# State products of a decayed delta rule: 40 stationary columns over cleared rows, and another order of the steps

## The chip, the cores and the metric

The kernel runs on one core of one Trainium2 chip. The metric is device microseconds (us) of the whole program. A core has TensorE (PE in the profile; its loads of the stationary operand are a row of their own, PEld), VectorE (DVE), ScalarE (ACT), GpSimd (POOL) and SyncE (SP), which issues nearly all DMAs. TensorE reads both operands from SBUF and writes to PSUM.

## What is computed

For each of 4 x 8 heads a 40 x 40 state is carried over 768 tokens; the outputs then pass a small gated network.

```python
for t in range(S):
    y[:, :, t] = einsum('bhd,bhde->bhe', rt, state)
    Sa = einsum('bhde,bhe->bhd', state, at)
    state = state * wt[:, :, None, :] - einsum('bhd,bhe->bhde', Sa, bt) \
            + einsum('bhd,bhe->bhde', vt, kt)
# x: (4, 768, 320), all heads' y side by side
h = maximum(x @ w_in, 0)                 # 320 -> 1024
conv_out = 3-tap convolution of h along the tokens, a weight per channel
out = (h * sigmoid(conv_out)) @ w_out    # 1024 -> 320
```

All arrays are f32, and so are nearly all products.

## The kernel before, in words

The 768 tokens are cut into 24 steps of 32 tokens; two steps make a pair (12 pairs, `pds`) and also a window of the network (12 windows, `wds`). Each unit of work is a Python generator that issues some instructions and then yields: `load_wakb`, `decays`, `decayed`, `scores`, `solve_in`, `solve` per pair or step (they prepare the triangular systems of a step), `chain` (the recurrence), `hats`, `vturn`, `rturn`, `sturn`, `pairs`, `from_state`, `outputs`, `finish` (the attention output), `moe_pack`, `moe_in`, `moe_out` (the network) and the 23 pieces that decode the weights from 64-bit floats on DVE, seven instructions a piece (`wi..`, `wo..`, `wp..`, `cv` in tile names).

`ORDER` is a written list of 1990 tokens, such as `ch5*2`: "advance unit chain 5 by two yields". The order of tokens is the order of instructions on every engine and queue; nothing else schedules them. An engine takes its instructions in that order, so an instruction that waits holds all that stand behind it on its engine.

The recurrence of step n is `chain(st, nxt)`: products `pp` of the old state with `a64` (line 592) and of `vu` with `at` (line 603); a copy to `psb`; products `pu` with `tt`, the solved system (line 618); copies of `pu` into `vu` on ACT (line 631) and DVE (line 629); then the **state product** `pn` (line 644); the DVE addition to the old state (line 655, line 653 in step 0); and the POOL multiplication by the decay (line 660), on which the next step's line 592 waits. There are 23 state products: the last step has none.

The state lies in rows 0 to 39 (even heads) and rows 64 to 103 (odd heads) of `states`; line 655 works on all of rows 0 to 103. Each state product has, per head, two batches `y` and two row halves `z` (partitions 0 to 63 and 64 to 127 of `kb` and `vu`), 32 products of 40 moving columns, each of which appears as two instructions in the profile. For even heads the stationary operand has 64 columns (`m = D if x else 64`, D being 40): the 24 further ones belong to the next head and fill rows 40 to 63 of `pn` with finite numbers that nobody uses, so that line 655 reads nothing that was never written. For odd heads it has 40.

`solve` is 62 instructions that depend on one another, on DVE for the pairs whose letter in `SOLVER` is v and on POOL for the others. Its input goes through DRAM (`bd`, then `bb`), and so does its output (`xd`, then `tt`).

Of the kernel before, what the change touches and what calls it, by code (L numbers as in the profile page):

```python
# [39 lines left out]
st1 we9 st1 we5 so1 dd2 pa0 si1 we9 ld2 we10 vt0 ch1*2 so1 vt1 dd2 pa0 vt1 ou0 rt0 we9 so1 we10 ld2  # L40
we10*2 dd2 so1*2 dd2*2 ch1 lr1 dd2 ou0*2 ld2 we11 we12 lv2 we6 ch1 sc4*2 ha2 we10 sc4 sc5 ld3 st1
pa0 ha2 fs1 we11*2 sc5 de2 we12 de2 fs1 de2 fi0 pa1 so1 vt1 we13 ha2 ha3 fi0 ch1*2 ha3 de3*2 ld3
we9 pa1 ou1 rt1 we12 fi0 ha3 fi0 dd2 fi0 we13 si2 ou1 ch2 fi1 ou1 we12 rt1 fi1 st2 pa1 we14 ch2 de3
st2 de3 so1 fi1 so1 so2 we11 ch2 ha4 fi1 so2 we15 ch2 we14 ch2 fs2 ha4 de3 we15 ch2*2 vt2 we16
ro0*2 pk0 mi0.0 so2 st2 rt1 fs2 lv3 ch2 vt2 so2 we16 mi0.0 dd3 ch2 mi0.1 ha4 we17 ch3 dd3 so2 we17
mi0.0 ch3*2 mi0.1*2 ld3 st3 mi0.0*2 we18 st3 lv2 ch3 de3 ch3 pa2 dd3 vt2 ld3 ha5 we19 ld3 vt3 pa2
vt3 ld4 fi1 ou2 vt3 we18 ch3 we19 st3 ou2 lr2 ha5 ch3 so2 mi0.1 pa2 mi0.1 lv4 mi0.1 mi0.2 dd3 mi0.1
ou2 fs3*2 pa3 ha5 dd3*2 so2 we20 we21 pa3 lv5 mi0.3 fi2 ou3 fi2 dd3 sc5 so2 fi2 mi0.1 lv1 ou3 mi0.0
ch3 sc6 mi0.3*2 ch3 st4 mi0.0 sc6 so2 we20 si2 fi2 st4 ch4*2 sc6 ch4 mi0.3 fi2 mi0.0 fi3 rt2 mi0.0
fi3*2 mi0.3 rt2 we21 dd3 mi0.2*2 sc7 ch4 sc7 we22 de4 lr0 ch4*2 lr1 mi0.2 we2 mi0.3 ch4 mi0.2*2  # L50
we22 mi0.2 mi0.3*2 mi0.2 mo0.1 we20 mi0.1 fi3 pk1 mo0.1 de4 vt4 mi1.0 mi1.1*3 si3 lv3 mi0.3 ou3
mi1.0 ch4 ld4 lv5 ld4 so2 de4 mo0.0 mi1.0 so3*2 mi1.1*2 so3 ch4 fi3 sc7 we14 ld4 pa3 lv6 st4 fs4
ch5*2 vt4 mo0.1 dd4 mi1.1 mi1.0 si3 mi1.0 we16 we1 pk1 vt4 ch5 so3*3 mo0.1 mi1.1 lr3 dd4*2 mi0.2
mi1.1 fs4 ha6 pa4 ld4 mi1.3 pa4 ha6 dd4*3 ou4 mi1.3 dd4 mo0.1*2 mi1.3 st5 so3 pa4 st5 ld5 mo0.0
we18 dd4 mi1.3 sc8 mi1.0 sc8 mi1.3 sc8 mi1.0 sc9 ou4 ro0 sc9 ch5*2 st5 mi1.0 mi1.2*3 mi1.3 so3
vt5*2 mi1.2*2 si4 ou4 ch5 so3 mi1.2 ch5 mo0.0 ha6 ha7 mo0.0 ha7 ch5 fs5*2 pa5 mi1.2 sc9 mo0.0 mi1.2
ch5 de4*3 fi4 de5 mi1.3 mo0.0 pa5 so3 de5 ou5 so4 rt2 ou5 de5 fi4*2 mi1.3 fi4 mo1.1 rt3 fi4 mo1.0
fi5 rt3 vt5 fi5*3 ch6*2 ou5 pa5 mo1.1*2 de5 so4 ch6*2 de5 ch6 st6 mo1.0 st6 ch6 pk2 mi1.3 vt6 mo1.1
so4 we12 mi1.2 mi2.2*2 lv7 ch6*3 lv8 so4 vt6 ha7 ch7 fs6*2 pa6 ld5 st6 so4 mo1.0 pa6 si4 mi2.2 st7
ld5 we7 mi1.0 fi5 rt3 ch7 st7 ch7 so4 ld5 mi2.3*3 vt6 ha8 ou6 so4 ha8 so4 ou6 mo1.1 ch7*2 dd5*2 we8  # L60
ch7*2 dd5 ou6 pa6 ch7 mi2.2 mi2.3 fi6*2 mi1.1 vt7 dd5 mi2.0 mi2.2 vt7 fi6*3 we3 fs7 ch7 vt7 mi2.3
ch8 mi2.2*2 pk0 lr4 dd5 mi2.2 ha8 fs7 ch8*2 dd5 mi2.0*2 mo1.0 so4 dd5 de5 mi2.3 sc10*3 sc11 st7
mi2.0 ld5 ld6 mi2.0 st8 mi2.3 sc11 ha9 ch8 ld6 st8 we13 st8 mi2.0 ch8 mi2.3 ha9 pa7 de6 si5 pa7 ld6
lv9 de6 ch8*2 pa7 ou7*2 sc11 dd5 ch8 so4 rt4 de6 fi7 lr4 fi7*2 rt4 vt8 fi7 so5*3 mo1.1 vt8 pk3
mi2.1*4 ou7 so5 mi2.1*2 lv9 dd6 mi2.0 mi2.1*2 ld6 fs8*2 pa8 we15 lv8 ha9 mo1.0 vt8 we22 ld6 ld7 de6
mo1.0 mi2.1 de6 pa8 mi2.0 mi2.2 si5 mi3.1*3 mi3.2 ch8 ch9*2 dd6*2 de6 so5*2 ch9 mo2.1 pk2 dd6*3
mi3.2 mi3.1 we21 ou8 dd6 mi3.1 mi3.2 mi3.1 ou8 we17 dd6 lv10 st9*2 sc12*2 st9 pa8 sc12 sc13 mi2.3
fi7 ld7 sc13 ch9 mi3.1 rt4 ch9 so5 lr5 mi3.2 ou8 mi3.1 de7*3 mi3.3 fi8 mi3.3*2 vt9 mo2.1 si6 ha10
fi8 vt9 mi2.0 fs9*2 pa9 so5*2 ch9 mi3.3*2 mi3.2 fi8 so5 we19 pa9 ha10 mo2.1*2 ou9 ch9*2 vt9 ou9*2
lv6 fi8 mo2.1 fi8 mi3.2*2 ha10 rt5 mi3.0 mo2.0 so6 mi3.2 rt5 mo2.1 mi3.0 ld7 lr2 ch9 mi3.0 fi9  # L70
ch10*3 so6 mo2.0 st10 mi3.2 mi3.0*2 mo2.0 ch10 st10 ld7 ha11 fi9 mi3.3 fi9 ch10 mi3.0 ch10 ha11
ch10 mi3.1 mi3.0 so6 ha11 fi9 mi3.3 mo2.0 mi3.3 pk4 ch10 lr3 vt10 lv11 dd7 ch10 fs10 vt10 mi3.0
ch11 mi3.0 mi3.3 mi4.0*3 mo3.1*2 mi4.0 dd7 so6*2 mi4.0 ch11 vt10 mi4.0 lr6 so6 pa9 mi4.2*3 ch11
fs10 dd7 fi9 de7 ld7 mo2.0*2 de7 ch11 mi4.0 ch11 st10 ha12 st11*2 mi4.2 pa10*2 mo3.1 ha12 pa10
mi4.2 so6 dd7 ou10 mi4.2 ch11 ou10 mi4.3 mo3.1 de7 mo3.0 rt5 fi10 dd7 so6 fi10*3 ch11 fi10 we11
# [926 lines left out]
```

## Time and profile before

| | |
|---|---|
| median of 3 runs | 658.02 us (656.59 to 660.3) |
| the profiled execution | 654.06 us |
| its span, first to last instruction | 652.3 us |
| PE busy | 565.5 us, 87% of the span |
| DVE, POOL, ACT busy | 474.7, 289.7, 281.0 us |
| mean granted TensorE clock, as a share of full speed | 0.922 |

The profile is of one execution, so sums of its rows stand against 654.06 us, of which 1.8 us lie outside the span. Matmuls are pipelined: busy PE says that some product was under way, not that the engine ran at its peak. "issue" as a releaser means that the engine waited for nothing that the profile shows. A row gives the line of the program, the engine, the operation, and out<-in by the program's names.

### The profile page before, as it was taken

The numbers are of one execution on the slowest core, as the hardware profiler recorded it, in microseconds if no ns is written. First come the engines' busy times: TensorE is split into PE (matmuls) and PEld (weight loads), VectorE is DVE, ScalarE is ACT, GpSimd is POOL, SyncE is SP. The second block draws the span as 40 slices with busy tenths as digits, with TensorE's granted clock in tenths as the row PEclk, the third lists the DMA queues.
The fourth block names the chain that finished last, engine by engine and source line by source line (L and its number), as shares of the span: only waits on it lengthen the run. The fifth ranks groups of instructions, "written<-read, shape, count | busy, mean of one in ns | idle before, by whom it ended". The sixth has DMA issues, their size and how long they took to land.

```text
span 652.3 us, 31811 instructions
## 1 busy us (share of the span) xinstructions
PE 565.5 (87%) x14385; PEld 486.4 (75%) x14385; DVE 474.7 (73%) x977; ACT 281.0 (43%) x578; POOL 289.7 (44%) x530
## 2 busy tenths in 40 slices
PE   3536677888799999989998998988999998999998
PEld 2535566787688788877887887867977887788884
DVE  7899978789968987767975458966658985254552
ACT  2112223355436254545525446514535426456562
POOL 5030488884786211884012772010687125851000
PEclk9866687798989998989997999989999988999999
DMA  9592835582923566534522652552763522120011
GB/s 145 80 155 35 154 65 115 127 149 56 122 53 70 89 110 96 96 72 73 92 51 59 95 93 49 80 98 41 114 88 70 95 53 55 39 55 21 12 26 31
DMA packets 214400, 51.89 MB, mean 80 GB/s; under 512 B 203729, under 2 KB 208809, under 8 KB 214265
## 3 DMA queue, kind: packets, MB, share of 16 engines
q1 hardware_dynamic: 210104, 49.20, 44.3%
q8 instruction: 113, 1.85, 1.2%
q10 hardware_dynamic: 4160, 0.66, 0.8%
q14 instruction: 23, 0.18, 0.1%
HBM read 38.30 MB, written 10.22 MB: 74 GB/s over the span
## 4 chain that ended last, share of the span: by engine, by line
PE 40%; POOL 23%; DVE 21%; issue 9%; DMA 6%; SPq 1%; ACT 0%; POOLq 0%; DVEq 0%; ACTq 0%
POOL st L560 11%; PE po L846 10%; POOL xx L566 9%; PE ph L799 9%; DVE xx L566 4%; DVE st L560 4%; PE pm L709 2%; PE ps L498 2%; DVE cc L828 2%; PE pu L618 2%; DMA bb<-bd 2%; PE pn L644 2%; DVE k L481 2%; PE pt L694 1%; DMA bd<-at 1%
## 5 line engine op out<-in xcount | busy, mean ns | idle before, releaser
L846 PE MATMUL po<-wo,g 128*128 128x320 f32 x384 | 121.1, 452 | 0.0
L828 DVE SCALAR_TENSOR_TENSOR cc<-hb,cw,cc 128x256 f32<-128x256 f32 x192 | 93.0, 546 | 38.5 <-ACT cc L820 38.3
L560 POOL TENSOR_TENSOR st<-xx,bb 128x126 f32<-128x126 f32 (+22 forms) x217 | 100.5, 463 | 20.6 <-DMA bb<-bd 4.2
L566 POOL TENSOR_TENSOR xx<-xx,st 128x126 f32<-128x126 f32 (+22 forms) x217 | 94.7, 436 | 17.0
L846 PEld LDWEIGHTS po<-wo,g 128*128 128x128 f32 x384 | 70.3, 197 | 22.9 <-issue 2.2
L660 POOL TENSOR_TENSOR state<-state,a 104x640 f32<-104x640 f32 x23 | 36.7, 1597 | 112.4 <-DVE state L655 106.5
L776 POOL TENSOR_TENSOR xl<-xf,xh 120x384 fp32r<-120x384 f32 x24 | 28.7, 1196 | 119.3 <-ACT xf L774 119.3
L799 PE MATMUL ph<-xh,wih 120*128 120x256 f32 x288 | 74.9, 320 | 0.1
L813 ACT ACTIVATE hb<-ph 128x512 f32<-128x512 f32 x48 | 28.7, 598 | 72.8 <-PE ph L799 72.6
L799 PEld LDWEIGHTS ph<-xh,wih 120*128 120x128 f32 x288 | 50.7, 199 | 4.1 <-issue 0.5
L566 DVE TENSOR_TENSOR xx<-xx,st 128x56 f32<-128x56 f32 (+22 forms) x155 | 46.0, 297 | 5.3
L833 ACT ACTIVATE cc<-cc 128x512 f32<-128x512 f32 x48 | 29.8, 630 | 41.5 <-DVE cc L828 40.7
L560 DVE TENSOR_TENSOR st<-xx,bb 128x56 f32<-128x56 f32 (+22 forms) x155 | 42.6, 275 | 5.2
L838 DVE TENSOR_TENSOR g<-cc,hb 128x512 f32<-128x512 f32 x48 | 34.4, 722 | 13.5 <-ACT cc L833 12.9
L820 ACT ACTIVATE cc<-hb,cw 128x256 f32<-128x256 f32 x96 | 43.5, 503 | 0.0
L799 PE MATMUL ph<-xh,wil 120*128 120x256 f32 x192 | 40.5, 294 | 0.2 <-issue 0.2
L799 PE MATMUL ph<-xl,wih 120*128 120x256 f32 x192 | 40.6, 294 | 0.0
L498 PE MATMUL ps<-a,k 40*64 40x32 f32 x1536 | 30.8, 230 | 10.7 <-issue 8.1
L498 PEld LDWEIGHTS ps<-a,k 40*64 40x64 f32 x1536 | 28.4, 146 | 14.4 <-issue 11.2
L644 PE MATMUL pn<-vu,kb 64*64 64x40 f32 (+1 forms) x1472 | 30.4, 221 | 7.8 <-DVE vu L629 2.3
L644 PEld LDWEIGHTS pn<-vu,kb 64*64 64x64 f32 (+1 forms) x1472 | 26.4, 127 | 12.6 <-issue 4.3
L716 DVE TENSOR_TENSOR ms<-pm,tri 128x512 f32<-128x512 f32 x24 | 16.5, 687 | 25.8 <-PE pm L709 25.5
(286 smaller groups left out, 1186.1 us busy)
## 6 DMA issues: line engine op xcount, KB each, us to landing
bb<-bd SPq DMA_DIRECT2D x24, 256.0 KB
rin<-in_r_dram SPq DMA_DIRECT2D x48, 80.0 KB
vu<-in_v_dram SPq DMA_DIRECT2D x96, 40.0 KB
in<-in_w_dram SPq DMA_DIRECT2D x23, 160.0 KB
in<-in_a_dram SPq DMA_DIRECT2D x23, 160.0 KB
in<-in_k_dram SPq DMA_DIRECT2D x23, 160.0 KB
in<-in_b_dram SPq DMA_DIRECT2D x23, 160.0 KB
out_dram<-ob SPq DMA_DIRECT2D x44, 80.0 KB
```

The source lines that it names most:

```text
L498: nc.tensor.matmul(ps[half(z), x, (4 * y + i) * C : (4 * y + i) * C + C], pd["k64"][half(x, D), 2 * i + y, c, z], pd["a64"][half(x, D), re ...
L560: eng.tensor_tensor(t3, xx[:, 0:nj, i : i + 1].to_broadcast([128, nj, nt]), bb[:, i : i + 1, i + 1 :].to_broadcast([128, nj, nt]), ALU.mult,)
L566: eng.tensor_tensor(xx[:, 0:nj, i + 1 :], xx[:, 0:nj, i + 1 :], t3, ALU.add)
L644: nc.tensor.matmul(pn[half(x, m), z, q * D : q * D + D], kf[half(z), kp : kp + m], vu[half(z), h, y, 0:D], start=True, stop=True, skip_gro ...
L660: nc.gpsimd.tensor_tensor(new, new, al.to_broadcast([SR, 2, 8, D]), ALU.mult)
L776: nc.gpsimd.tensor_tensor(wd["xl"][:, :, :, tw], xf, xh.bitcast(F32), ALU.subtract)
L799: nc.tensor.matmul(ph[:, j], l[:, fs], x, start=(j == 0 and i == 0), stop=(i == len(passes) - 1), skip_group_check=True,)
L820: nc.scalar.activation(out=cc[:, j], in_=hb[:, j, :, 1 : W + 1], func=AF.Copy, scale=cw[:, 1, f : f + 1],)
L828: nc.vector.scalar_tensor_tensor(out=cc[:, j], in0=hb[:, j, :, x : W + x], scalar=cw[:, x, f : f + 1], in1=cc[:, j], op0=ALU.mult, op1=ALU ...
L833: nc.scalar.activation(out=cc, in_=cc, func=AF.Sigmoid)
L838: nc.vector.tensor_tensor(g, cc, hb[:, :, :, 1 : W + 1], ALU.mult)
L846: nc.tensor.matmul(po[:rows, :DM], parts(f), wo[:, f, :], start=(f == 0), stop=(f == NF - 1))
```

## The change

Every state product now has 40 stationary columns, for even heads too. As nothing fills rows 40 to 63 of `pn` any longer, two bf16 products of zeros go ahead of it, one for each row half `z`: 64 stationary columns from a new tile `zst` of zeros, and 320 moving columns of `xini`, a bf16 tile of ones and zeros that is there already. They write zeros into rows 0 to 63 of both banks; the even heads' products then overwrite rows 0 to 39.

```diff
+    zst = cp.tile([128, 64], BF16, name="zst")
+    nc.gpsimd.memset(zst, 0.0)
...
         pn = banks(f"pn{n}")
         kf = kb.rearrange("p q d -> p (q d)")
+
+        for z in range(2):
+            nc.tensor.matmul(
+                pn[half(0), z, 0:HD], zst[half(z)],
+                xini.rearrange("p s t -> p (s t)")[half(z), 0:HD],
+                start=True, stop=True, skip_group_check=True,
+            )
         for h in range(H):
             x, i = h % 2, h // 2
-            m = D if x else 64
             for y in range(2):
                 kp, q = kbp(h, y) * D, 2 * i + y
                 for z in range(2):
                     nc.tensor.matmul(
-                        pn[half(x, m), z, q * D : q * D + D],
-                        kf[half(z), kp : kp + m], vu[half(z), h, y, 0:D],
+                        pn[half(x, D), z, q * D : q * D + D],
+                        kf[half(z), kp : kp + D], vu[half(z), h, y, 0:D],
                         start=True, stop=True, skip_group_check=True,
                     )
```

The table `ORDER` is another one, with the same 1990 tokens in other places. Its first row shows the kind of difference:

```diff
-we0 ld0 we1 we0 we1 ld0 we0 ld0 de0 we2 de0 we0 de0 dd0*5 ld0 we2 dd0*2 de0 we3*2 de0 we0 sc0*3 sc1
+we0 we1 we0 ld0*3 we1 we0*2 we2 de0*3 dd0*5 we2 we3 ld0 dd0*2 de0 ld0 de0 we3 sc0*3 sc1 ld1 we2 de0
```

Lines of the changed kernel are numbered up to 7 higher. Three places show what moves.

On PE, around the state product of step 2 (`pn2`), with `py2` and `pv2` its neighbours. Before:

```order
L731 MATMUL py2_1766<-sd2_1633,r64_113 32x40 x32
L644 MATMUL pn2_1810<-vu0_117,kb2_1333 64x40 x4
L644 MATMUL pn2_1810<-vu0_117,kb2_1333 40x40 x4
L669 MATMUL pv2_1844<-ident_78,vu0_117 128x128 x8
L799 MATMUL ph00_1862<-xh0_1419,wih_127 128x256 x2
```

The two rows of `pn2` stand there four times in turn. Now:

```order
L738 MATMUL py2_1780<-sd2_1664,r64_115 32x40 x32
L641 LDWEIGHTS zst_98
L641 MATMUL pn2_1825<-xini_94,zst_98 64x320
L651 MATMUL pn2_1825<-vu0_119,kb2_754 40x40 x32
L676 MATMUL pv2_1883<-ident_78,vu0_119 128x128 x8
```

The rows of line 641 stand there twice, once for each row half. All 32 products of `kb` and `vu` have 40 columns, and the zeros are in front of them.

On PE, just ahead of the first products of step 3's chain (`pp3` from `state1`, which wait for POOL); `ph00` and `ph01` are the first products of the network. Before:

```order
L418 MATMUL pa3_1911<-ident_78,in1_107 128x128 x8
L799 MATMUL ph01_1920<-xh0_1419,wih_127 128x256 x2
L799 MATMUL ph01_1920<-xh0_1419,wil_128 128x256 x2
L799 MATMUL ph01_1920<-xl0_1420,wih_127 128x256 x2
L799 MATMUL ph01_1920<-xh0_1419,wih_127 128x256
L799 MATMUL ph01_1920<-xl0_1420,wil_128 128x256
L592 MATMUL pp3_1933<-state1_125,a641_397 32x40 x32
```

Now:

```order
L806 MATMUL ph00_1896<-xh0_1271,wih_129 128x256 x2
L806 MATMUL ph00_1896<-xh0_1271,wil_130 128x256 x2
L806 MATMUL ph00_1896<-xl0_1272,wih_129 128x256 x2
L806 MATMUL ph00_1896<-xh0_1271,wih_129 128x256
L806 MATMUL ph00_1896<-xl0_1272,wil_130 128x256
L806 MATMUL ph01_1916<-xh0_1271,wih_129 128x256 x2
L806 MATMUL ph01_1916<-xh0_1271,wil_130 128x256 x2
L806 MATMUL ph01_1916<-xl0_1272,wih_129 128x256 x2
L806 MATMUL ph01_1916<-xh0_1271,wih_129 128x256
L806 MATMUL ph01_1916<-xl0_1272,wil_130 128x256
L593 MATMUL pp3_1930<-state1_127,a641_411 32x40 x32
```

The transposes `pa3` went behind `pp3`, and the second eight products of `ph00`, which stood behind `pp3`, went ahead of it; a first group of eight stands ahead of these rows in both orders.

On DVE, at the end of pair 0's solve (`st0`, `xx0`), the second half of pair 1's scores (`at2` from `ps3`). Before:

```order
L505 TENSOR_TENSOR at2_568<-ps3_603,tris_89 128x2x2x128
L560 TENSOR_TENSOR st0_28_653<-xx0_399,bb0_361 128x45
L566 TENSOR_TENSOR xx0_399<-xx0_399,st0_28_653 128x15x3
L560 TENSOR_TENSOR st0_29_656<-xx0_399,bb0_361 128x30
L566 TENSOR_TENSOR xx0_399<-xx0_399,st0_29_656 128x15x2
L560 TENSOR_TENSOR st0_30_659<-xx0_399,bb0_361 128x16
L566 TENSOR_TENSOR xx0_399<-xx0_399,st0_30_659 128x16
L264 TENSOR_SCALAR wi21q_447<-wi21r_446 80x256
```

Now:

```order
L265 TENSOR_SCALAR wi02q_623<-wi02r_622 120x256
L269 TENSOR_SCALAR wi02q_623<-wi02r_622 120x256
L273 SCALAR_TENSOR_TENSOR wi02q_623<-wi02r_622,wi02q_623 120x256
L277 SCALAR_TENSOR_TENSOR wi02q_623<-wi02q_623 120x256
L278 TENSOR_SCALAR wi02q_623<-wi02q_623 120x256
L279 SCALAR_TENSOR_TENSOR wi02q_623<-wi02r_622,wi02q_623 120x256
L282 TENSOR_TENSOR wi02q_623<-wi02q_623 120x256
L506 TENSOR_TENSOR at2_545<-ps3_635,tris_89 128x2x2x128
L432 SCALAR_TENSOR_TENSOR suf_105<-wz_100,dp0_102 128x1056
```

`at2` from `ps3` moved from ahead of the last six instructions of the solve to behind the two weight pieces `wi21` and `wi02`.

## Rows read from the trace of the kernel before

**Rows 1.** The page: engines; PE, its clock and the DMA rate in 40 slices.

```profile
PE 565.5 (87%) x14385; PEld 486.4 (75%) x14385; DVE 474.7 (73%) x977; ACT 281.0 (43%) x578; POOL 289.7 (44%) x530
PE   3536677888799999989998998988999998999998
PEclk9866687798989998989997999989999988999999
GB/s 145 80 155 35 154 65 115 127 149 56 122 53 70 89 110 96 96 72 73 92 51 59 95 93 49 80 98 41 114 88 70 95 53 55 39 55 21 12 26 31
```

**Rows 2.** Busy time of each engine in six stretches of the span.

```profile
core 0: us, PE busy (x) PEld busy (x) DVE busy (x) ACT busy (x) POOL busy (x), PEclk, DMA share, GB/s
0.00:65.00 65.00, 31.27 (x544) 27.90 (x544) 56.58 (x139) 14.08 (x20) 16.51 (x32) 0.79 0.73 104
65.00:130.00 65.00, 49.64 (x1351) 43.56 (x1351) 53.88 (x100) 19.69 (x34) 50.00 (x99) 0.74 0.58 115
130.00:260.00 130.00, 118.47 (x3432) 103.66 (x3433) 109.55 (x220) 60.20 (x124) 66.34 (x117) 0.96 0.55 93
...
520.00:652.30 132.30, 125.60 (x2724) 103.28 (x2722) 67.35 (x141) 64.99 (x148) 39.88 (x73) 0.97 0.17 37
```

**Rows 3.** Waits of PE over the whole span: in total, times, longest, in us.

```profile
PE ps L498 <- issue: 8.1, 6, 3.0
PE pp L603 <- issue: 8.0, 3, 3.5
PE pp L592 <- POOL state L660: 7.3, 4, 4.1
PE pn L644 <- DVE vu L629: 2.3, 3, 1.9
```

**Rows 4.** Timeline of PE, single products: start, length, instructions, idle before with releaser.

```profile
592.64 1.13 PE L644 MATMUL pn<-vu,kb 64*64 64x40 f32 x64
552.96 0.79 PE L744 MATMUL py<-kb,ms 64*32 64x40 f32 x64
```

**Rows 5.** Groups by form, whole span: count, busy us, mean ns, idle before.

```profile
L644 PEld LDWEIGHTS pn<-vu,kb 64*64 64x64 f32 x736 | 26.3, 138 | 11.9 <-issue 3.6 <-DVE vu L629 3.3 <-ACT vu L631 1.5
L644 PEld LDWEIGHTS pn<-vu,kb 64*40 64x40 f32 x736 | 21.1, 117 | 0.7 <-issue 0.7
```

**Rows 6.** The chain that ended last: products of 320 and 256 moving columns.

```profile
577.20 1.08 PE po L846 x4
578.28 0.95 PE ph L799 x8
```

**Rows 7.** Timeline of PE, ACT and DVE in the first 20 us.

```profile
7.32 1.94 PE L418 MATMUL pw<-ident,in 128*128 128x128 f32 x8 [7.32 <-DMA in<-in_w_dram]
9.29 1.01 ACT L428 COPY wz<-pw 128x1024 f32<-128x1024 f32 x1 [0.43 <-PE pw L418]
12.24 2.35 DVE L431 TENSOR_TENSOR_SCAN suf<-wz,dp 128x1056 f32<-128x1056 f32 x1
```

**Rows 8.** Timeline of DVE, SP's queue and POOL, end of solve 0 to solve 1.

```profile
58.18 0.68 DVE L505 TENSOR_TENSOR at<-ps,tris 128x512 f32<-128x512 f32 x1
65.54 2.35 DVE L431 TENSOR_TENSOR_SCAN suf<-wz,dp 128x1056 f32<-128x1056 f32 x1
65.97 1.03 SPq L539 DMA_DIRECT2D bd<-at  x2
75.86 1.34 POOL L660 TENSOR_TENSOR state<-state,a 104x640 f32<-104x640 f32 x1
77.14 0.67 POOL L553 CAST xx<-xini 128x512 f32<-128x512 bf16 x1
```

**Rows 9.** Timeline of PE ahead of step 3's chain.

```profile
127.77 1.04 PE L418 MATMUL pa<-ident,in 128*128 128x128 f32 x8
131.24 0.82 PE L592 MATMUL pp<-state,a 40*32 40x40 f32 x64 [1.49 <-POOL state L660]
```

**Rows 10.** Waits of PE from 130 to 260 us.

```profile
PE pp L592 <- POOL state L660: 2.2, 2, 1.5
```

**Rows 11.** Timeline of PE at one of its longest waits on issue.

```profile
427.15 0.33 PE L731 MATMUL py<-sd,r 64*32 64x40 f32 x10 [3.30 <-issue]
428.49 3.84 PE L846 MATMUL po<-wo,g 128*128 128x320 f32 x7
```

More of the change, by code (lines that the diff above doesn't have):

```diff
@@ L40 @@
[L40 to L75, printed above, removed]
@@ new lines @@
+mi4.0 lv12 st11 dd7 mo3.0 dd7 pa10 mi4.2 we19 vt11*2 ch11 ou10 lv13*2 so6 mi4.2 pa10 mo3.1 mi4.1
+ch11*2 ou10 ha12 ch11 fi9 fi10 dd7 fi10*2 mi4.0*2 dd7 ou10 mi3.3 fs11*2 pa11 rt6*2 mi4.0 pa11 mi4.1
+mi4.2 mi4.1 ou11*2 rt6 ou11 fi10*2 sc14*2 st11 sc14 sc15*2 vt11 de7 dd7 mi4.2*3 de8*2 st12 pk3
+so6*2 st12 mi4.3*3 ha13 mi4.3 ch12*2 mo3.0 fi11 pa11 mo3.0 ch12 ha13 si6 ld8 mo3.1 fi11*2 si7*2
+mi4.1 ch12 fs12 fi11 pk5 de8 mi4.3*3 ch12 mi4.1 de8 mo3.0 de8 mi4.3*2 ch12*2 so7 ch12 st12 ld8*2
+ha13 mi5.3 so7 mi5.3*2 ch12 vt12 mi4.0 vt12 so7 mi4.1 so7 fs12 ch13 lv14 fi11 ch13*2 pa12 st13 dd8
@@ new lines @@
+mo4.0 ch14*2 mi5.1 lr8 ha16*2 pa13 mi6.3*2 ch14 mi5.2 mi6.3 so8 mo4.0 mi5.1 vt14 ch14 mo4.0 ch15*2
+pk5 vt14 pa14 vt14 ch15 pa14 ha17 st15 mi5.2*2 ch15*2 lv16 so8 ld9 so8 mi6.1 mo5.0 pk4 st15 vt15
+ou14*3 fs15 mo4.1 fs15 mi5.2 mo5.0*2 fi14 ha17 pa14 de9 vt15 ld9 mi6.1 ch15 dd9 ch15 mi6.1*3 dd9
+mi6.3*3 mo5.0 fi14 ld10 mi6.3 ch15 pa15 lv17 de9 pa15 dd9 de9*2 so8 dd9 mi6.0 mi6.3 mi6.0 mi6.1
+ch15 mi6.0 ch16 fi14 ou15 ld10 ou15 ha17 fi14 ch16 mi6.0 fi14 fi15 mi6.0*2 mi6.1 ch16 fi15 mi6.2
+dd9 fi15 mi6.0 dd9 mo5.1*2 pa15 dd9 so8 mi6.1 vt15 mi6.1 mi6.2*3 dd9 sc17 ha18*2 sc18*3 sc19 mi6.0
@@ new lines @@
+sc21 ld11 de11 mi7.2 ou16 ch17*2 ou16*2 fs17 mi7.3 mo6.1 ld11 si10 vt17 ha19 mo6.0 vt17 fs17 so9
+dd10 pa17 ha19 pa17 mi7.1 mi7.2 mo6.0 rt9 st17 mi7.2 rt9 ou17 ch18*3 lv17 mi7.2 ha19 fi16 ou17
+fi16*4 ou17 ha20 st18 so9 mi7.2 so10 st18 so10 fi17*2 mo6.0*2 mo7.0*2 ha20 fi17 pa17 fi17 lr8 ha20
+de11 rt9 ch18*2 fi17 mo7.0*2 de11 ch18 mi7.1 mi7.0 so10 lv19 vt17 ch18 so10 ch18 fs18 st18 pk8
+mi8.0*3 vt18 ch18 vt18 ch19*2 dd11 mo7.0 ld11 lr10 ch19 lr10 sc21 mi8.0 lv20 so10 dd11*4 mi8.0
+ch19*2 si10 dd11*2 fs18 pa18 so10 st19*2 sc22*3 sc23 mi8.3*3 ch19 sc23 pa18 mi8.3 si11 mo6.1 mo7.1
@@ new lines @@
+ou20 mi8.2 ch21*2 lr11 mi9.0 fi20 mi9.2 mi9.0*2 mo8.0 mi9.0 mi9.2 fi20*2 lv22 ch21 so11 mi9.0*2
+ch21 mi9.1 mi9.2*2 mi9.1 lr11 vt21 mi9.2 mi9.1 lv23 mi9.3 so11 mo8.0 mi9.1 vt21 mo8.1 mi9.1 so11
+ou20 fs21 mi9.1 fs21 pa21 mi9.1 pa21 mi9.2 lv20 lv21 ch21 mi9.1 so11 mi9.3*2 mo8.1 ch21 ch22 ou21*2
+ch22 mi9.3 fi20*2 fi21 mo8.1 mi9.3 mi9.0 mi9.3 fi21 mi9.2 fi21*2 mi9.3 ch22 mi9.3 mi9.2 pk10
+mo8.1*3 mo9.1*2 mi9.1 ha22 st21 ch22 st22 ha22 ch22 rt11 mi10.1 pa21 st22 ch22*2 vt21 mi10.1 rt11
+mi10.1 mi9.2 mi10.1 ou21 ch22 mi10.0 ha22 fs22 mi10.0 lr9 rt11 st22 mi9.3 ch22 fs22 ch23 mi10.0
@@ new lines @@
+vt22 mo9.1 mi10.0*2 vt22 mi10.0 mo9.1 ch23 mi10.1 pa22 ch23 vt22 pa22 lv18 mi10.0 mi10.1 ch23*2
+ha23 st23 ha23 mi10.1*2 st23 mi10.3*2 mo9.0 mi10.3 pa22 mi10.0 mi10.3*2 fi21 ha23 pk10 vt23 mo9.0
+lv23 vt23 ou22*3 vt23 mi10.3 mo9.1*2 fs23*2 pa23*3 mo9.0*2 fi22*3 ou23*3 fi22 mi10.3 lv22 dd11
+mo9.0*2 mi10.2*2 mi10.1 fi22 fi23 de11 mi10.0 fi23*3 sc23 mi10.3 mi10.2*6 mo10.0*2 ld11 mo10.1*2
+mi10.2 pk11 ch23 mi10.3 mi11.1*3 st23 mi11.1*5 mi11.0*4 pk11 mi11.0*2 mi11.2 mo10.0*2 mi11.2*2
+mo10.0 mi11.0*2 mo10.0 mi11.2*2 mi11.3*3 mi11.1 mi11.3 mi11.2 mi11.3*2 mo10.1*2 fi23 mi11.2*2
@@ L124 @@
+mo10.1*2 mi11.3*2 mo11.0*4 mi11.2 en0 lr7 mi11.3 mo11.0*2 mo11.1*5 en0 mo11.1 en0 mi11.0
 """
```

108 lines of the change are left out of this document (56 added, 52 removed).

## The prediction, made before the changed kernel was run

> **What bounds the kernel now.** I read the page first. PE is busy for 87% of the span, DVE for 73%, POOL for 44% [rows 1], so the question is where PE's gaps lie. The row of 40 slices shows them ahead of the tenth slice, some 160 us; from there it mostly reads 8 or 9. The six stretches give the sizes [rows 2]: PE is busy for 31.3 of the first 65 us, 49.6 of the next 65, then 118.5 of 130, and 125.6 of the last 132.3. In the first stretch DVE is busy for 56.6 of 65 us, in the second POOL for 50.0 of 65. So there are three parts: up to about 77 us DVE sets the pace (it decodes weights and solves pair 0), up to about 150 us DVE and POOL together (POOL solves pairs 1 and 2), and from then on PE, which is short of nothing but its own time and what it waits for.
>
> The waits of PE then tell which of its gaps another order could close [rows 3]. The longest kinds are "issue" in the middle of a product (8.1 us on line 498, 8.0 on line 603): no tile is missing there, so no order of tiles shortens them on purpose. Of the waits on other engines the largest on the recurrence is that of line 592 on POOL's state, 7.3 us in 4 waits. Just 2.3 us are waits of the state product for DVE's copy of vu.
>
> **The state product, the part that the diff shows.** A clean one takes 1.13 us for its 64 instructions [rows 4]; there are 23. The nearest product with fewer stationary columns and the same 40 moving ones is py, 32 columns: 0.79 us for 64 instructions [rows 4]. These are the two ends: with 40 columns for all heads the product costs between 0.79 and 1.13 us. Even heads now have 40 columns instead of 64, and 40 lies nearer to 32, a quarter of the way from 32 to 64: 0.79 + 0.34 x 8/32 = 0.875. I take 0.85, a little under, as half of the columns were 40 already in the 1.13. That is 0.28 us less for each, 23 x 0.28 = **6.4 us**.
>
> Does the number of columns set the pace at all? The loads of 64 columns last 138 ns on the mean, those of 40 columns 117 ns [rows 5]: 21 ns for 24 columns. The Trainium skill, "TensorE: Matmul & The Clock Gate", section "LDWEIGHTS (loading the stationary operand)", gives the load time as the columns divided by 1.2, in ns, which would be 20 ns for 24 columns; by that, the trace agrees. What the row does not say is how much of this lies on the path, since loads of two row halves and two column halves overlap: 64 instructions in 1.13 us are 17.7 ns apart, and those of py 12.3 ns apart, both far below the length of one load.
>
> The same page speaks against a large gain, in its section on a gap of 56 ns where 53.3 were expected: starts of products do not come closer than about 25 ns, however few columns move. One at a time that would make 1.6 us of 64 instructions, which the trace contradicts (1.13); with two row halves at once it would make 0.80 us, near to py's 0.79. By that rule the sum would have 0.33 us for each product at best, 7.6 us in all, against my 6.4.
>
> **The zeros.** The trace has no bf16 product. Each of the two has 320 moving columns. The nearest rows are the network's [rows 6]: eight instructions of 256 columns in 0.95 us, 0.119 us each, so 0.149 us for 320 columns; and four f32 ones of 320 columns in 1.08 us, 0.27 us each. Lower end: the two overlap, as they lie on different row halves and write different banks: 0.15 us. Upper end: f32's pace, one after the other: 0.54 us. In between: one after the other at the first pace, 0.30 us. I take 0.15, because the state product itself shows its row halves at work together: at the f32 pace of 0.27/320 = 0.84 ns a column, 64 instructions of 40 columns would need 2.16 us in turn, and take 1.13. Cost 23 x 0.15 = **3.4 us**; at the ends 3.4 and 12.4. The zeros need only the bank, so where the product waits for vu they run in the wait; with 2.3 us of such waits in all this is worth little, and I count nothing for it. Two tails remain uncounted: the first f32 product must follow bf16 ones (no row shows that change), and the memset of zst on POOL, 64 columns, which stands among start-up memsets while PE waits 7.32 us for its first DMA [rows 7].
>
> Sum of the edit: -6.4 + 3.4 = -3.0 us, and this counts in full where PE sets the pace, which is the part after 150 us; of 23 products about 18 lie there, and on the others the chain is shorter by as much.
>
> **The order.** Three places, each with its row.
> - Start: on SP's queue a second weight piece (wi10, 240 KB) goes ahead of the first w. At the 145 GB/s of the first slice [rows 1] that is 1.7 us. PE's first product would start that much later; ACT's copy ends at 9.29 + 1.01 = 10.30, and DVE takes it at 12.24, after the piece wi10 [rows 7]. 1.94 us of cover: nothing. If the cover were gone, the whole DVE part would shift by the rest.
> - DVE at the end of solve 0: at2 moves behind two weight pieces. The six solve instructions behind it start 0.6 us earlier, the two pieces end as much earlier, and at2 ends where suf began, at about 65.6 us. The DMA bd that carries it to solve 1 is issued at 65.97 [rows 8], behind tt on SP. Nothing again. Solve 1 on POOL starts at 77.14 behind the multiplication of state 0 [rows 8], whose predecessors on DVE and POOL keep their order; so the first 77 us stay as they are, within a microsecond.
> - PE ahead of step 3's chain: PE idles 1.49 us for POOL's state [rows 9]. Now eight more products of ph (0.95 us, [rows 6]) stand ahead of the wait, and the transposes pa (1.04 us long, [rows 9]) behind it. These nearly cancel; pa then serves DVE later by about as much.
>
> The rest is hundreds of small moves. What they can win on purpose is bounded by the waits on other engines after 130 us: the largest of these is line 592's for POOL's state, 2.2 us between 130 and 260 us [rows 10]; the others are below that each. What they can lose is bounded by nothing as simple: moved DMAs meet "issue" waits elsewhere. One wait of 3.30 us shows the price [rows 11]: behind it seven products of 320 columns took 3.84 us, 0.55 each against 0.27, so the clock was at its lower level, 1.2 GHz, for a stretch, and the stall cost about 3.3 + 1.9 us. I count **-1.0 us** for the order, half of 2.2, with -6 and +6 (one such stall gone or added) as ends.
>
> **Sum.** -3.0 - 1.0 = -4.0 us. The profiled execution, 654.06 us, would become 650.1; it lies 4 us under the median 658.02, below all three timed runs, so I put the same -4.0 to the median: **654.0 us**, 0.6% faster. A measurement of this kernel can tell about 0.5% from no change, 3.3 us, so this lies just beyond it.
>
> **Rivals.**
> 1. *No change that can be told.* The product does get shorter, but as much goes to the zeros (0.30 instead of 0.15 gives 6.4 - 6.9 = +0.5 us), or the order gives back the rest. For it: the bounds of the two prices overlap, and PE's waits leave the order little. Against it: nothing certain. Time 657.5 us.
> 2. *Slower: the zeros hold the column half.* The zeros use the 64 columns that the even heads' products need next, so if they run in turn and at the f32 pace (0.54 us), the pair and the product take 0.54 + 0.85 = 1.39 us against 1.13: 23 x 0.26 = +6.0 us, 664.0 us. It decides from 0.28 us for the pair on. For it: no row shows a bf16 product beside f32 ones. Against it: ph's pace, and the overlap of row halves.
> 3. *Loads set the pace.* If the 32 long loads are one chain, 32 x 21 ns = 0.67 us go from each product, which leaves 0.46, with zeros 0.61: 23 x -0.52 = -12.0 us, 646.0 us. For it: [rows 5]. Against it: py with fewer columns still takes 0.79.
> 4. *The change does not do what it says.* The order printed for the changed kernel shows 40 columns in all rows and two zero products; I give this no chance of its own.
>
> **How the numbers follow.** Forecast 654.0, taken as faster: 0.37. Rival 1: 0.36. Rival 2: 0.17. Rival 3: 0.10. Faster by over 0.5%: 0.37 + 0.10 = 0.47; within 0.5%: 0.36; slower: 0.17. The range reaches down to rival 3 (646.0) and up to 662.0, where a smaller form of rival 2 or one further stall on top of rival 1 (657.5 + 4.5) ends. It leaves out most of rival 2. The forecast's own range, by the order's ends, is 649 to 660.
>
> **What would show it.** In the changed profile a clean state product with its zeros should take about 1.0 us on PE, with the zeros' two instructions at the same start; over 1.13 would refute the first step. DVE's and POOL's first 77 us should be unmoved to 1 us, with solve 1 starting between 76 and 78 us. Line 592's waits on POOL should be between 5 and 8 us. If the sum of "issue" waits on PE moves by more than 5 us, the order's effect was in DMA traffic and not in the waits that I counted. A time below 648 or above 662 would say that a term is missing.

## The result, and the profile after

The changed kernel takes 650.12 us (median of 20 runs, 643.92 to 703.02), the kernel before 656.96 us (median of 20, 650.3 to 660.3): a ratio of 0.988, interval 0.985 to 0.991. The forecast was 654.0 us and faster; the time lies inside the range and is 3.9 us better. (A few runs of a kernel lie far above its others, such as the 703; ratios leave them out.) The profiled execution of the changed kernel took 652.08 us, its span is 650.0 us against 652.3 before.

The page of the changed kernel first: the engines, PE's granted clock in 40 slices, and one of its DMA queues (packets, MB, share of 16 engines).

```profile
PE 558.1 (86%) x14431; PEld 480.4 (74%) x14431; DVE 476.0 (73%) x977; ACT 280.6 (43%) x578; POOL 287.6 (44%) x531
...
PEclk9675587779999699999998999998998999989999
...
q8 instruction: 113, 1.85, 1.2%
```

PE has 46 products more than in [rows 1], the two of zeros in 23 steps, and is busy 7.4 us less. The third line, of a queue for instructions, matters further down. The same stretches as in [rows 2], the last but for its end:

```profile
0.00:65.00 65.00, 30.82 (x536) 27.66 (x536) 57.55 (x141) 11.36 (x18) 14.59 (x32) 0.71 0.67 113
65.00:130.00 65.00, 49.27 (x1365) 43.47 (x1365) 53.07 (x96) 22.73 (x39) 49.80 (x99) 0.69 0.48 104
130.00:260.00 130.00, 114.92 (x3285) 99.59 (x3286) 105.10 (x217) 57.16 (x118) 65.93 (x116) 0.92 0.46 89
...
520.00:650.00 130.00, 121.38 (x2618) 99.88 (x2606) 64.79 (x139) 63.92 (x145) 37.22 (x73) 0.99 0.18 37
```

Up to 130 us PE has done as much work as before (80.1 us busy for 80.9). From 130 to 260 us it is busy for 114.9 us instead of 118.5, with 147 products fewer: the place where it falls behind is there. Next the product and its surroundings, from the timeline (start, length, instructions, idle before with releaser), in order of time.

```profile
8.49 1.94 PE L419 MATMUL pw<-ident,in 128*128 128x128 f32 x8 [8.49 <-DMA in<-in_w_dram]
12.31 2.35 DVE L432 TENSOR_TENSOR_SCAN suf<-wz,dp 128x1056 f32<-128x1056 f32 x1
...
64.28 0.68 DVE L506 TENSOR_TENSOR at<-ps,tris 128x512 f32<-128x512 f32 x1
64.88 2.35 DVE L432 TENSOR_TENSOR_SCAN suf<-wz,dp 128x1056 f32<-128x1056 f32 x1
64.99 0.92 SPq L540 DMA_DIRECT2D bd<-at  x2
...
76.41 0.67 POOL L554 CAST xx<-xini 128x512 f32<-128x512 bf16 x1
...
213.88 0.95 PE L593 MATMUL pp<-state,a 40*32 40x40 f32 x64 [7.13 <-POOL state L667]
...
436.73 0.76 PE L604 MATMUL pp<-vu,at 32*32 32x40 f32 x61
439.81 0.27 PE L604 MATMUL pp<-vu,at 32*32 32x40 f32 x3 [2.33 <-issue]
...
590.73 0.32 PE L641 MATMUL pn<-xini,zst 64*64 64x320 bf16 x2
590.89 0.87 PE L651 MATMUL pn<-vu,kb 64*40 64x40 f32 x64
591.70 0.50 PE L806 MATMUL ph<-xh,wih 120*128 120x256 f32 x2
```

The last three rows are a clean state product. It begins with its zeros at 590.73, the f32 instructions follow 0.16 us later, and PE turns to ph at 591.70: 0.97 us from start to next start (of the 23, 18 run through like this, with a median of 0.96). Before, the row behind the one in [rows 4] is this:

```profile
593.70 0.50 PE L799 MATMUL ph<-xh,wih 120*128 120x256 f32 x2
```

593.70 - 592.64 = 1.06 us, which is also the median of the 15 that ran through there. So a step gains **0.09 us** on PE, 23 x 0.09 = 2.1 us, not the 3.0 that I summed. The groups by form answer to [rows 5]: all loads of the product are now of 40 columns.

```profile
L651 PEld LDWEIGHTS pn<-vu,kb 64*40 64x40 f32 x1472 | 21.4, 119 | 2.4 <-DVE vu L630 1.5 <-issue 0.3
L641 PE MATMUL pn<-xini,zst 64*64 64x320 bf16 x46 | 7.6, 327 | 0.0
```

They last 119 ns where the two kinds had 138 and 117; the zeros never wait (0.0). The waits of PE (in total, times, longest, in us) show what else moved.

```profile
PE pp L593 <- POOL state L667: 15.2, 7, 7.1
PE pp L604 <- issue: 4.2, 2, 2.3
PE pn L651 <- DVE vu L630: 0.9, 3, 0.4
```

All rows of PE's waits added up by kind: "issue" 30.8 us before and 17.9 now, waits on other engines and DMAs 51.8 before and 70.9 now. With the busy time the spans' difference closes: -7.4 - 12.9 + 19.1 = -1.2 of the -2.3 us. The stretch from 130 to 400 us shows the exchange: "issue" falls from 14.0 to 5.2 us, and line 593, which before waited 2.2 us for POOL's state there, waits 10.8, of it 7.13 at 213.88 us (the row above). PE was through with what stands ahead at 206.75 us there, where before it came at 210.87 and did not wait; but POOL multiplied that state 7 us later. Before, then now:

```profile
205.56 1.29 POOL L660 TENSOR_TENSOR state<-state,a 104x640 f32<-104x640 f32 x1
```

```profile
212.53 1.29 POOL L667 TENSOR_TENSOR state<-state,a 104x640 f32<-104x640 f32 x1
```

Ahead of it on POOL stands a solve, which began 2.4 us later (at 173.15 instead of 170.79 us) and took 39.4 us instead of 34.8. So PE was earlier and POOL's chain later; why the solve took longer isn't shown.

### The profile page after: what moved, and what is told of

The parts are those of the page before. It is cut to its first block, busy times and chain, and to the rows that moved or that the text cites. A ratio compares the mean times of both kernels' runs of the same rounds, so it can differ in the third digit from the quotient of the medians.

```text
span 650.0 us, 31881 instructions
## 1 busy us (share of the span) xinstructions
PE 558.1 (86%) x14431; PEld 480.4 (74%) x14431; DVE 476.0 (73%) x977; ACT 280.6 (43%) x578; POOL 287.6 (44%) x531
## 3 DMA queue, kind: packets, MB, share of 16 engines
q8 instruction: 113, 1.85, 1.2%
## 4 chain that ended last, share of the span: by engine, by line
PE 36%; POOL 29%; DVE 19%; issue 14%; DMA 2%; ACT 1%; SPq 0%; POOLq 0%; DVEq 0%; ACTq 0%
POOL st L561 12%; POOL xx L567 11%; PE po L853 10%; PE ph L806 6%; DVE st L561 4%; DVE xx L567 4%; POOL state L667 3%; PE pp L604 2%; PE pt L701 2%; PE pm L716 2%; PE pp L593 2%; PE pu L619 1%; PE ps L499 1%; DVE vu L630 1%; PE pq L771 1%
## 5 line engine op out<-in xcount | busy, mean ns | idle before, releaser
L561 POOL TENSOR_TENSOR st<-xx,bb 128x126 f32<-128x126 f32 (+22 forms) x217 | 97.9, 451 | 19.2 <-DMA bb<-bd 2.8
L567 POOL TENSOR_TENSOR xx<-xx,st 128x126 f32<-128x126 f32 (+22 forms) x217 | 98.3, 453 | 17.0
L783 POOL TENSOR_TENSOR xl<-xf,xh 120x384 fp32r<-120x384 f32 x24 | 24.8, 1032 | 100.5 <-ACT xf L781 100.5
L806 PEld LDWEIGHTS ph<-xh,wih 120*128 120x128 f32 x288 | 49.3, 194 | 5.8 <-issue 1.3
L567 DVE TENSOR_TENSOR xx<-xx,st 128x56 f32<-128x56 f32 (+22 forms) x155 | 47.7, 308 | 5.3
L845 DVE TENSOR_TENSOR g<-cc,hb 128x512 f32<-128x512 f32 x48 | 33.9, 709 | 14.4 <-ACT cc L840 10.8
L630 DVE COPY vu<-pu 32x320 f32<-32x320 f32 x48 | 23.5, 491 | 22.0 <-PE pu L619 21.0
L806 PE MATMUL ph<-xl,wih 120*128 120x256 f32 x192 | 39.2, 286 | 0.0
L593 PE MATMUL pp<-state,a 40*32 40x40 f32 x1472 | 18.8, 216 | 17.8 <-POOL state L667 15.2
L693 ACT COPY v<-pv 128x1024 f32<-128x1024 f32 x24 | 24.2, 1010 | 22.1 <-PE pv L676 22.1
```

Of the source, the lines that this page charges most:

```text
L561: eng.tensor_tensor(t3, xx[:, 0:nj, i : i + 1].to_broadcast([128, nj, nt]), bb[:, i : i + 1, i + 1 :].to_broadcast([128, nj, nt]), ALU.mult,)
L567: eng.tensor_tensor(xx[:, 0:nj, i + 1 :], xx[:, 0:nj, i + 1 :], t3, ALU.add)
L593: nc.tensor.matmul(pp[quad(bi), x, i * D : i * D + D], a64[half(x, D), rec(h, y, z, c), 1:], old[half(x, D), z, 2 * i + y, 0:D], start=(i ...
L630: nc.vector.tensor_copy(dst, src)
L806: nc.tensor.matmul(ph[:, j], l[:, fs], x, start=(j == 0 and i == 0), stop=(i == len(passes) - 1), skip_group_check=True,)
L845: nc.vector.tensor_tensor(g, cc, hb[:, :, :, 1 : W + 1], ALU.mult)
```

## Experiments

### The two parts alone

The first runs took the parts apart. e1_edit_alone is the changed kernel with the order of before:

```diff
 ORDER = """
-we0 we1 we0 ld0*3 we1 we0*2 we2 de0*3 dd0*5 we2 we3 ld0 dd0*2 de0 ld0 de0 we3 sc0*3 sc1 ld1 we2 de0
+we0 ld0 we1 we0 we1 ld0 we0 ld0 de0 we2 de0 we0 de0 dd0*5 ld0 we2 dd0*2 de0 we3*2 de0 we0 sc0*3 sc1
...
```

> The order of before with the new state product (40 columns behind two bf16 products of zeros). Theory A (the product carries what was forecast, and the order the rest): a clean product with its zeros takes 1.03 us on PE against 1.13, 23 x 0.095 = 2.2 us, so 0.3% faster than before, 655 us beside 657. Theory B (the product carries nearly all of the 6.8 us, through shorter latency on the recurrence or less contention): 650 to 651 us. Theory C (the product's part is lost beside other work, the order is everything): 657 us.

e2_order_alone is the changed kernel without the edit:

```diff
-        for z in range(2):
-            nc.tensor.matmul(
-                pn[half(0), z, 0:HD], zst[half(z)],
...
+            m = D if x else 64
...
-                        kf[half(z), kp : kp + D], vu[half(z), h, y, 0:D],
+                        kf[half(z), kp : kp + m], vu[half(z), h, y, 0:D],
```

> The new order with the state product of before (64 columns for even heads, no zeros). Theory A: about 4.6 us faster than before, 0.7%, 652 us. Theory B: 656 to 657 us, no change. Theory C: 650 us, as fast as the whole change. In the profile, by A and C the waits of PE on issue should be near 18 us in total (31 before), by B near 31.

Measured: the edit alone 650.79 us, ratio 0.989 (0.983 to 0.994); the order alone **640.28 us**, ratio 0.974 (0.969 to 0.979). By the medians the edit gains 6 us from the kernel before and the order 17; together they gain 7. On top of the new order the edit costs 10 us. No sum of terms gives this, my own included, and none of the theories A to C had 640 us for the order alone: something depends on both.

### The product by itself

e3_odd_first leaves the zeros' columns for last, so that the first f32 instructions need not wait for them:

```diff
-        for h in range(H):
+        for h in (1, 0, 3, 2, 5, 4, 7, 6):
```

> The whole change, but odd heads go first in the state product. Their column half is free while the zeros stream through the other one. If column halves work independently, the first odd products start within 0.03 us of the zeros instead of 0.16 us, and the product with its zeros takes about 0.92 us instead of 1.03: 23 x 0.11 = 2.5 us less than the change, 647.5 us beside 650. If products start strictly in order behind the zeros, 1.03 us and no difference.

e4_zeros_f32 clears the bank at f32's pace:

```diff
-    zst = cp.tile([128, 64], BF16, name="zst")
+    zst = cp.tile([128, 64], F32, name="zst")
...
-                xini.rearrange("p s t -> p (s t)")[half(z), 0:HD],
+                vu[half(z)].rearrange("p h y d -> p (h y d)")[:, 0:HD],
```

> The whole change, but the zeros and their moving operand are f32 (zeros times the first 320 columns of vu, so that they wait for vu as well). The second rival of the prediction had 0.54 us for such a pair, if the row halves run in turn. If the two overlap at f32 pace, 0.27 us instead of 0.15: 23 x 0.12 = 2.8 us over the change, 653 us. If in turn, 23 x 0.39 = 9 us, 659 us. If microseconds of PE are not what ends the program, no difference.

Timeline of PE in e3_odd_first, then in e4_zeros_f32, one clean product each:

```profile
585.66 0.32 PE L641 MATMUL pn<-xini,zst 64*64 64x320 bf16 x2
585.67 0.94 PE L651 MATMUL pn<-vu,kb 64*40 64x40 f32 x64
586.54 0.39 PE L806 MATMUL ph<-xh,wih 120*128 120x256 f32 x1
```

```profile
606.60 0.76 PE L641 MATMUL pn<-vu,zst 64*64 64x320 f32 x4
607.19 0.87 PE L651 MATMUL pn<-vu,kb 64*40 64x40 f32 x64
607.99 0.51 PE L806 MATMUL ph<-xh,wih 120*128 120x256 f32 x2
```

Odd heads first, the product starts 0.01 us behind the zeros and all takes 0.88 us: half of the zeros' price is gone. The f32 zeros are four instructions and hold the product back by 0.59 us: 1.39 us in all, 0.42 more than the bf16 ones. Both agree with the working of the prediction; rival 2's 1.39 us is e4's to the hundredth, though as 0.59 and 0.80 instead of 0.54 and 0.85. But the times don't follow the product: e3 takes 650.04 us, where 23 x 0.09 = 2 us less than the changed kernel's 650.12 was due, and e4 664.57 us (ratio 1.010, 1.004 to 1.016), 14.4 us more where 23 x 0.42 = 9.7 were due.

### Where PE stops

"Issue" is a wait in the middle of a product, for nothing that the profile names. To see where it falls, PE's instructions in each trace are numbered from 0 in order of start: a weight load and a product each, and the semaphore instructions. Before, the stop of [rows 11] stands in front of instruction 19137, and 19137 = 74 x 256 + 193. The others too: of 22 stops of over 0.3 us inside one tile's products, 21 have the number 192 or 193 modulo 256 (the remainder when it is divided by 256). The page says what comes in such portions: the instruction queue carries 113 packets with 1.85 MB, 16 KB each, and PE has 28,917 instructions, close to 113 x 256 = 28,928. In all 14 profiles of this study 228 of 251 such stops stand at 192 or 193; of the other 23, 20 lie before 73 us, at two products that wait there for DVE.

The traces hold the time of each of these packets, and they settle what PE waits for. The stop of [rows 11] lasts from 423.85 to 427.15 us. Within it, from 424.2 to 425.9 us, one packet crosses the instruction queue (packets, MB, share of 16 engines):

```profile
q8 instruction: 1, 0.02, 5.8%
```

It lands at 425.81 us, and PE goes on 1.34 us later. It is so everywhere. In the 14 profiles PE passes 1570 such borders, not counting the first of each, at 192. At every one of them packet k has landed before instruction 256k + 192 starts, by 1.19 us or more, and the 228 stops end 1.21 to 1.88 us behind their packet (the middle half 1.35 to 1.49).

So **theory D**: PE's instructions come to it in blocks of 256, and where PE runs through a block faster than the next one comes, it stands at the border. Whether the border falls into 64 small instructions of 0.8 us together or among long ones of po and ph depends on the count of all PE instructions ahead of it, which the change raises by two a step and which a new order deals out anew. The rival, E, was that the zeros themselves cost or gain the time. To shift the borders and nothing else, tiny products of zeros go ahead of PE's first transposes, where PE waits for its first DMA; the transposes overwrite what they write:

```diff
+        for _ in range(88 if nm == "w" and pd["j"] == 0 else 0):
+            nc.tensor.matmul(
+                ps[0:32, 0, 0:1], zst[0:64, 0:32], zst[0:64, 0:1],
+                start=True, stop=True, skip_group_check=True,
+            )
```

88 and 44 of them in the changed kernel, 40 in the order alone, 64 in the kernel before (with zst, where that has none):

> The whole change, with 88 tiny bf16 products of zeros (32 stationary columns, one moving column) put ahead of PE's first transposes, where PE waits for the first DMA; each is two PE instructions. The waits on issue stand, in every profile so far, 128 products (256 instructions) or a multiple of it apart, and the zeros' 46 further products move these places. Theory D (PE waits there for its own instructions, which arrive in blocks of 256, so the place of the blocks' borders in the program matters): the change has 40 to 46 more products than the new order alone in the last third, so 88 more bring the borders to 128 products from there, where the new order alone has them. Waits on issue in the last third go from 8.8 us to under 2, and the time comes to 638 to 642 us. Rival E (the new order suffers from the zeros themselves: their bank, their place ahead of the product): no change, 650 us.

> The new order with the state product of before, and 40 tiny products at the start. Theory D: the borders of the last third come to where the whole change has them; waits on issue rise from 7 to about 16 us, and the time from 640 to about 648 us. Rival E: 640 us as without the 40.

> The whole change with 44 tiny products at the start: borders at places that no kernel so far had. Theory D: another sum of waits on issue, anywhere from 7 to 33 us by the kernels so far, and a time that moves with it, microsecond for microsecond in the last third. Rival E: 650 us.

> The kernel before with 64 tiny products at the start, half a block. Theory D: its waits on issue (31 us, the most but one of the kernels so far) stand at unlucky places, and elsewhere the sum is likelier to be smaller: 10 to 25 us, and a time 4 to 12 us under before's. Rival E: before's time, within 0.5%.

The waits of PE on "issue" in e8_before_pad64 are these four kinds, and no more:

```profile
PE pp L457 <- issue: 2.1, 2, 1.6
PE ps L506 <- issue: 1.8, 2, 1.6
PE pp L611 <- issue: 0.8, 2, 0.6
PE py L752 <- issue: 0.7, 2, 0.3
```

That is 5.4 us, where the kernel before has 30.8, of it 16.1 in the first two rows of [rows 3].

Measured: e5_change_pad88 **636.39 us** (ratio 0.967, 0.962 to 0.972), e6_order_pad40 **662.41** (1.006, 1.002 to 1.010), e7_change_pad44 652.87 (0.988, 0.982 to 0.994), e8_before_pad64 **633.51** (0.963, 0.959 to 0.966). Instructions that do nothing take 23 us from the kernel before, more than any other version here, and add 22 us to the order alone. The zeros of the change can't do this, as e8 has no change in it and e6 none of the edit. D gave the direction but no size: e6 lost more than it had allowed, e5 and e8 gained more, and e7 has 8.3 us more of waits on issue than the change with 2.8 us more of time.

### The control: one whole block

If the place of the borders is the cause, 128 tiny products (256 instructions) must undo what 64 do, as every border then falls where it fell before. If it were early work on PE, or its clock, they must do at least as much.

```diff
-        for _ in range(64 if nm == "w" and pd["j"] == 0 else 0):
+        for _ in range(128 if nm == "w" and pd["j"] == 0 else 0):
```

> The kernel before with 128 tiny products of zeros ahead of PE's first transposes, 64 more than in e8_before_pad64. 128 products are 256 PE instructions, one whole block. Theory D (what counts is where in the program the borders of 256 PE instructions fall): every border falls where it falls in the kernel before, so the gain of 23 us is gone: 653 to 660 us, an issue total of PE of 26 us or more, with waits in front of the same products as before (among them line 498's ps at some 25 us, the pp at 175 and the py at 424 us). Theory E (work on PE during the first load, or a later start, is what helps): at least the gain of e8, 628 to 636 us, and an issue total under 8 us.

Measured: **654.97 us**, ratio 0.999 (0.995 to 1.002). The gain is gone, and the waits on issue are back, 31.6 us of them. Here is the same product py of line 731 in three kernels: before, e9 (128 tiny products) and e8 (64), timeline of PE, each time its first rows to where it goes on; before, the row that follows is in [rows 11].

```profile
423.03 0.82 PE L731 MATMUL py<-sd,r 64*32 64x40 f32 x53
```

```profile
424.19 0.70 PE L739 MATMUL py<-sd,r 64*32 64x40 f32 x53
427.80 0.47 PE L739 MATMUL py<-sd,r 64*32 64x40 f32 x10 [2.90 <-issue]
```

```profile
415.72 0.90 PE L739 MATMUL py<-sd,r 64*32 64x40 f32 x63
416.56 1.15 PE L717 MATMUL pm<-r,v 128*64 128x64 f32 x32
```

Before and in e9 PE stops with 10 instructions of the product left, 3.30 and 2.90 us; in e8 it runs through. The pages' instruction queues (packets, MB) of e9 and of e8 agree, one packet more for 256 instructions and none for 128:

```profile
q8 instruction: 114, 1.87, 1.2%
```

```profile
q8 instruction: 113, 1.85, 1.2%
```

A clock raised by the early work is not the cause: granted in the stretch from 14 to 65 us it was 0.73 before, 0.67 in e9 and 0.74 in e8.

### The new product with the borders moved

Last, e1_edit_alone with 24, 40 and 56 tiny products (the diff as above with these numbers), to see whether the product's own gain shows once the borders lie well.

> The new state product in the old order, with 24 tiny products ahead of PE's first transposes. Two more products in each of 23 steps make 46 by the end, so after 400 us the program stands 24 + 36 to 46 = 60 to 70 products later against the borders than in the kernel before, nearly where e8_before_pad64 has it (64); before 130 us only 24 to 34. Theory D: no issue wait after 400 us, as in e8, some earlier, and the shorter product worth its 23 x 0.09 = 2 us: 629 to 638 us. If instead the new product costs something by itself (the zeros on DVE's or PE's chain): above 640 us even with no issue wait after 400 us.

> As e10_edit_pad24 with 40 tiny products: against the borders 40 to 50 products later than before in the first 130 us, 76 to 86 after 400 us. Theory D: the early stretch as in e5_change_pad88 or better, few issue waits after 400 us (e5 has 88 plus the same 36 to 46 and none there): 630 to 645 us. If the place of the borders did not matter, this and e10_edit_pad24 would both stand at the 651 us of e1_edit_alone.

> The new state product in the old order with 56 tiny products, the last of the row 0, 24, 40. The edit's own two products a step are added: against the borders 56 products later than before at the start, some 64 to 84 between 100 and 350 us, where e8_before_pad64 (64) had few issue waits and e11_edit_pad40 (48 to 72) still 13, and 92 to 102 after 400 us, between e11's 76 to 86 and e5_change_pad88's 124 and more, both without long waits there. Theory D: 630 to 640 us, an issue total below e11's, and, if the shorter product shows in full, at or below the 633.5 us of e8. If offsets do not decide: about the 640 to 646 us of its two neighbours, or the 651 us of e1_edit_alone.

Measured: 645.85 us (ratio 0.980, 0.975 to 0.985), 640.48 (0.975, 0.970 to 0.979) and 636.96 (0.970, 0.965 to 0.974). The first misses its 629 to 638: after 400 us its waits on issue are gone as expected (0.9 us), but from 130 to 400 us there are still 16.3 us of them. Over 640 us without such waits after 400 us was to speak for a cost of the new product by itself; with 16.3 us ahead of that, where the expectation had "some", this run can't decide it. The two others are as expected, yet none reaches e8's 633.5.

All kernels in one table. "Stops" are those of over 0.3 us inside one tile's products at instruction 192 or 193 modulo 256, in the profiled execution (number, then sum).

| kernel | median us | span | stops |
|---|---|---|---|
| before | 656.96 | 652.3 | 21, 30.0 us |
| before + 128 (e9) | 654.97 | 651.0 | 24, 30.5 |
| before + 64 (e8) | 633.51 | 631.4 | 6, 4.9 |
| edit alone (e1) | 650.79 | 653.6 | 16, 24.4 |
| edit + 24 (e10) | 645.85 | 648.2 | 14, 18.4 |
| edit + 40 (e11) | 640.48 | 639.1 | 15, 17.9 |
| edit + 56 (e12) | 636.96 | 638.1 | 12, 11.7 |
| order alone (e2) | 640.28 | 642.5 | 9, 6.9 |
| order + 40 (e6) | 662.41 | 658.8 | 26, 30.3 |
| change | 650.12 | 650.0 | 13, 14.5 |
| change + 44 (e7) | 652.87 | 654.1 | 23, 25.1 |
| change + 88 (e5) | 636.39 | 634.4 | 11, 10.9 |
| odd heads first (e3) | 650.04 | 645.2 | 15, 15.3 |
| f32 zeros (e4) | 664.57 | 665.3 | 23, 30.6 |

In three pairs that differ in tiny products alone the median moves with the stops: 25.1 us of stops and 23.4 us of time between before and e8, 23.4 and 22.1 between e2 and e6, 12.7 and 13.8 between e1 and e12. In the family of the change it does not: e7 has 10.6 us more of stops than the change and 2.8 of time, e5 3.6 us less and 13.7 of time. So a kernel does not simply pay the length of its stops. Within one execution the sum closes only with all of PE's waits and its busy time. From before to e8 "issue" falls by 25.4 us, PE is busy 9.4 us less, and it waits 14.0 us more on other engines and DMAs: -20.8 of the span's -20.9 us. From the change to e5 the three are -5.4, -4.1 and -6.3: -15.8 of -15.6 us. A stop can stand in place of a wait for another engine, and it can cost more than its length: behind the stop of [rows 11], from 428.4 to 432.4 us, PE was granted 0.57 of its full clock. What is left without the stops: the median less their sum is 624.5 to 628.6 us for the three of the old order and product, 622.6 to 627.4 for the four with the edit, means 626.7 and 625.4. So the product's 2.1 us may be in there, but a spread of 4 us hides them.

## Why the prediction was right, and by which steps not

The time and the sign were right; **the split was not**, and part of the hit is luck: with other borders the same change would have come out between 636 and 653 us (e5, e7), and the 636 lies outside the range.

- *The state product, -6.4 us.* Too large. Without its zeros the f32 part runs from 590.89 to 591.70, 0.81 us to the next start, where the old one took 1.06: 0.25 for the forecast's 0.28 us, 5.8 us. The loads became narrower and shorter as forecast; that they alone make the gain, no run shows. The rule on loads in the prediction (the Trainium skill, "TensorE: Matmul & The Clock Gate", section "LDWEIGHTS (loading the stationary operand)") agrees with the trace in the difference alone, 20 against 21 ns; the loads' own 138 and 117 ns lie far above the 53 and 33 ns that it gives for 64 and 40 columns.
- *The rule set against it*, 25 ns between starts (the Trainium skill, "TensorE: Matmul & The Clock Gate", section "Wait — 56ns, not 53.3ns?"). By that rule and with two row halves at once starts are 12.5 ns apart. The product's 64 instructions lie in 0.87 us, of which the last takes 0.20: 0.67 us for 63 starts, 10.6 ns. The trace is a little below the rule so taken, and the measurement decides. A gain of the size that the rule allowed (0.33 us) still didn't come. The 17.7 ns of the old product were its length over 64; counted in the same way its starts are 14.3 ns apart (0.90 us for 63).
- *The zeros, +3.4 us.* Price right in kind: the two start 3 ns apart, and hold the product up by 0.16 us, 3.7 us. e4 shows the upper case, e3 how to halve the price.
- *The edit's sum, -3.0 us*: -2.1 by the timeline, from -5.8 and +3.7. This is the term that was mis-sized, and small beside what follows. The 1.0 us per product that was to be seen is 0.97.
- *The order, -1.0 us.* The step that failed. Alone it gave -16.7 us by the medians; on top of the edit -0.7 (650.12 against e1's 650.79), which can't be told from nothing. I bounded it by waits on engines and allowed -6 to +6 for "one such stall gone or added", taking stalls to come from DMA traffic. They came from where the borders of PE's instruction blocks fell.
- *Start and solve 0.* Right. PE's first product starts 1.17 us later (8.49 against 7.32 us in [rows 7], 1.7 forecast), the scan on DVE at 12.31 against 12.24; at now ends at 64.96 and bd is issued at 64.99, against 65.97 in [rows 8]; solve 1 starts at 76.41 us, between 76 and 78.
- *Line 592, now 593*, was to wait 5 to 8 us for POOL: wrong, 15.2 us, the longest behind a solve on POOL that took 4.6 us longer. That PE meets POOL's chain more where it is stopped less is only argued: e2 waits 18.5 us with 6.9 us of stops and e6 7.2 us with 30.3, but e7 waits 12.5 with 25.1, and e9 12.0 where before waits 7.3.
- *The check on "issue".* Its sum moved by 12.9 us, more than the 5 I had named; so the order's effect was not in the waits that I counted. My reading of it, DMA traffic, named the right place and the wrong traffic: what PE waits for is the packet with its own instructions, and e9, which moves no transfer in the program and no tile's order, has the stops back.
- *Rivals.* Rival 1's cause (zeros at 0.30 us) is refuted by 0.16; rival 2's is what e4 does, not the change; rival 3's by 0.81 us for the product, where it had 0.46.

What stays open: when the next packet is sent for. Over all 14 profiles a block that PE passed in under 3 us (its stop not counted) ended in a stop in 154 of 250 cases, one that took over 5 us in 4 of 676. What tells the short ones apart is their next packet: where its transfer began before PE was at the first instruction of the block, 4 of 79 ended in a stop, where it began later, 150 of 171. e8 has nearly as many short blocks as before (17 against 19) and a stop at 4 of them instead of 15; in 11 of them, against 3, the packet was under way early. Why it sets out early is not shown. Nor was it tried whether the new order is by itself slower once borders are equal; less their stops e2 and e6 lie at 633.4 and 632.1 us, some 6 us above the old order's three, which speaks for it.
